# Third experts of two neighbouring tiles as seven block products, their sums kept in PSUM, in a fused attention and expert kernel

## The chip, the cores and the metric

One core of a Trainium2 chip runs the whole program. The metric is the time of one execution in microseconds on the device; of several runs the median counts.

## The reference

```python
def sm_attn(qq, kk, vv):
    s = scale * np.matmul(qq, kk.transpose(0, 1, 3, 2))
    s = s - np.max(s, axis=-1, keepdims=True)
    a = np.exp(s)
    a = a / (np.sum(a, axis=-1, keepdims=True) + 1e-09)
    return np.matmul(a, vv)
p_packed = sm_attn(p, k, v)
out = sm_attn(q, p_packed, p_packed)
...
h = np.maximum(np.maximum(x @ w1, x @ w2), x @ w3)
return (h @ w_out).astype(np.float32)
```

There are 8 batches of 8 heads, 576 tokens and a head width of 64; p holds 32 packed queries per head. The attention's output, with its heads side by side, is the x (4608 tokens by 512) of the second part: three experts (512 by 768 each), their elementwise maximum, and an output matrix (768 by 512). Everything is float32.

## The kernel before, in words

**Products.** A float32 matrix is split into a high part that TensorE multiplies exactly and a low part (`hi`, `lo`); one product of two such matrices is three matmuls, hi by hi, lo by hi and hi by lo, added up in one bank of PSUM.

**The low rank.** x of a batch is A by P: A (576 tokens by 8 heads x 32 = 256) the weights of the second attention, P (256 by 512) the packed rows. So x @ w is A by (P @ w). P @ w for tile j, 128 columns of each expert, is the stage P, `project` (L444 to L500): 32 small matmuls (L459) into two banks r = 0, 1 of 3 x 128 columns. The product with A is the stage N, `layer_in` in the batches 0 and 1 and `layer_in_fast` (L535 to L577, matmuls in L543) in the batches 2 to 7. For one expert and one tile it has four block products: two halves r of the 256 by two halves of 288 tokens.

**Seven for eight.** In the fast batches the experts 0 and 1 of a tile share the blocks of A, so their eight products are written as seven with sums and differences of the blocks (Strassen's way): those of A are made once a batch (T, `th`, `tl`), those of P @ w by `combine` (L486) for every tile. The third expert has its four plain products: two into the bank `me`, two into `mf`. A tile so takes 11. Its five banks are joined to the maximum of both token halves by the stage E, `maximum_fast` (L579 to L609): three or four copies out of PSUM by ScalarE or VectorE (L148, L150), and six joins (L587), all on VectorE, into `r`, the tile pair's rows in SBUF.

**Layer-out.** H (`halves`, L664 to L683) makes hi, lo and differences of the pair's rows (`ya`, `yb`, `yc`), O (`layer_out_fast`, L784) multiplies them with `w_out` in seven products over 14 banks of nine matmuls, F brings them to SBUF and out. A pair is two neighbouring tiles; six tiles are three pairs.

**The attention.** Per batch: S scores of the packed queries, A softmax and turn, X spread, V values (L357) and their scaling by VectorE (L367), K: one transpose of the packed rows on TensorE (L372) and a copy of it (`pt`, L148), Q the second scores from `pt` (L386), B the second softmax, which gives A's hi and lo (`a2h`, `a2l`). P needs `pt` too.

**The order** is written by hand, in three lists of words: START (weights, batches 0 and 1, the beginning of 2), LOOP (once for each b = 2 to 6), LAST (batch 7). A word is a stage, its batch relative to b (left out in w, C, W, R), its tile or half, and perhaps an engine:

```python
            name = word.rstrip("vga")
            chosen[0] = word[len(name):] or None
            kind, x = name[0], [int(i) for i in name[1:]]
...
                next(begun[key], None)
```

Each word runs one step of its stage, up to the next yield. `v`, `g`, `a` put the step's operation on VectorE, POOL (GpSimd) or ScalarE where it has a choice; the joins have none. Every engine works its own queue in the order in which the words issue. k, v, q, w are loads, all on SP's queue. I and J set a number of filler units, matmuls of the identity on itself (`rouse`, L162), in front of the next product or at once.

**Memory.** PSUM has eight banks: two pairs for scores, values, projections, queries (`ps_big`), four single banks for layer-in and layer-out (`ps_moe`); the projections 3 and 4 of the fast batches take single ones. SBUF tiles share rings of 6, 8 and 21 places (NX, NB, NY), taken in the order in which they are asked for.

## Time and profile before

| | us |
|---|---|
| median of three runs | 459.67 |
| lowest, highest run | 457.22, 459.70 |
| span of the profiled execution | 454.8 |
| TensorE busy in it | 448.5 |
| VectorE, POOL, ScalarE busy | 389.0, 266.7, 253.7 |
| one batch of the loop | 52.66 |

The profile is one execution. An engine's busy time counts its instructions from start to end, so that where two overlap they count once; the groups by line add up single instructions and can be more. Matmuls are pipelined: one that lasts 0.30 us has its successor behind it after less. The stretch of a loop batch is read from the start of one batch's scores to the start of the next batch's. The profile's spans on POOL are rough.

### The profile page before, as it was taken

To read this page: it belongs to the slowest core of one execution; us is meant where nothing else is said; L and a number is where in the kernel's file an instruction comes from. 1 tells how busy PE (TensorE), PEld (TensorE's weight loads), DVE (VectorE), ACT (ScalarE), POOL (GpSimd) and SP (SyncE) were. 2 spreads that over 40 slices of the span, in tenths; PEclk is the share of its full clock that TensorE was granted. 3 is DMA by queue.
4 is the path that set the end of the run, shared out by engine and by line. 5 is a ranking of instruction groups with operands and counts; after the bars stand their busy time and mean duration, and the time that the engine had idled before them with its cause. 6 is when DMAs were issued, how large, how long until landed. Compare 5 with 4: busy or idle time off the path is not lost.

```text
span 454.8 us, 11856 instructions
## 1 busy us (share of the span) xinstructions
PE 448.5 (99%) x4616; PEld 391.0 (86%) x4616; DVE 389.0 (86%) x825; ACT 253.7 (56%) x552; POOL 266.7 (59%) x280
## 2 busy tenths in 40 slices
PE   8999999999999999999999999999999999999997
PEld 4467888899999888988899888998889888999897
DVE  1799997999998989887997889898898879977883
ACT  2786956674453547446483546655474464744540
POOL 0458775644617685746856486836856478553350
PEclk9999999999999999999999999999999999999999
DMA  8999937000435450163304551063502640020002
GB/s 315 398 386 370 330 66 275 2 0 1 140 109 169 111 178 1 61 208 90 128 0 134 161 144 48 27 203 81 175 1 79 192 95 4 1 105 1 1 2 104
DMA packets 35783, 55.68 MB, mean 122 GB/s; under 512 B 17296, under 2 KB 26512, under 8 KB 35728
## 3 DMA queue, kind: packets, MB, share of 16 engines
q1 hardware_dynamic: 35728, 54.93, 36.3%
q8 instruction: 36, 0.59, 0.5%
q14 instruction: 19, 0.16, 0.1%
HBM read 41.94 MB, written 9.44 MB: 113 GB/s over the span
## 4 chain that ended last, share of the span: by engine, by line
PE 82%; DMA 12%; SPq 3%; DVE 1%; ACT 1%; issue 1%; POOL 0%; POOLq 0%; DVEq 0%; ACTq 0%
PE mo L784 22%; PE mx L543 10%; PE me L543 9%; PE mo L707 7%; DMA wi<-in_wi 7%; PE mu L543 6%; PE pw L459 6%; PE mf L543 6%; PE mi L630 6%; PE my L543 3%; DMA q<-in_qt 3%; SPq L339 2%; DMA v<-in_va 2%; PE s L386 2%; PE av L357 2%; PE s L273 1%
## 5 line engine op out<-in xcount | busy, mean ns | idle before, releaser
L672 POOL TENSOR_TENSOR r<-r 128x288 f32<-128x288 f32 (+1 forms) x39 | 45.4, 1164 | 59.1 <-DVE r L672 22.9
L477 DVE SCALAR_TENSOR_TENSOR pl<-pw,ph 128x768 fp32r<-128x768 f32 (+1 forms) x61 | 46.7, 775 | 11.4 <-ACT ph L475 11.2
L486 POOL TENSOR_TENSOR pf<-pf 128x128 f32<-128x128 f32 x72 | 40.7, 576 | 10.1 <-ACT pf L469 6.8
L153 POOL TENSOR_TENSOR sl<-pf,sh 128x384 fp32r<-128x384 f32 x28 | 30.6, 1100 | 27.2 <-DVE sh L150 17.7
L630 PE MATMUL mi<-a2h,ph 128*128 128x288 f32 x144 | 44.1, 306 | 0.0
L630 PE MATMUL mi<-a2l,ph 128*128 128x288 f32 x144 | 42.5, 295 | 0.0
L630 PE MATMUL mi<-a2h,pl 128*128 128x288 f32 x144 | 42.4, 294 | 0.0
L475 ACT ACTIVATE ph<-pw 128x768 fp32r<-128x768 f32 (+1 forms) x61 | 40.0, 680 | 2.8 <-PE pw L459 1.9
L459 PE MATMUL pw<-w_sb,pt 64*32 64x384 f32 x768 | 39.1, 490 | 0.1
L469 ACT ACTIVATE pf<-pw 128x512 f32<-128x512 f32 (+1 forms) x48 | 22.3, 492 | 26.4 <-PE pw L459 26.3
L225 POOL TENSOR_TENSOR w_sb<-w_sb,wi 128x512 int32<-128x512 int32 x18 | 23.7, 1327 | 21.7 <-DVE w_sb L221 16.2
L543 PE MATMUL me<-a2h,ph 128*128 128x288 f32 x108 | 32.6, 302 | 0.0
L630 PEld LDWEIGHTS mi<-a2h,ph 128*128 128x128 f32 x144 | 27.0, 188 | 6.4 <-issue 3.0
L784 PE MATMUL mo<-ych,xh 128*128 128x288 f32 x108 | 32.1, 298 | 0.0
L784 PE MATMUL mo<-ych,xl 128*128 128x288 f32 x108 | 31.9, 295 | 0.0
L543 PE MATMUL me<-a2h,pl 128*128 128x288 f32 x108 | 31.8, 294 | 0.0
L543 PE MATMUL me<-a2l,ph 128*128 128x288 f32 x108 | 31.8, 294 | 0.0
L784 PE MATMUL mo<-ycl,xh 128*128 128x288 f32 x108 | 31.8, 294 | 0.0
L148 ACT COPY r<-me 128x288 f32<-128x288 f32 x35 | 14.2, 405 | 25.1 <-PE me L543 25.1
L630 PEld LDWEIGHTS mi<-a2l,ph 128*128 128x128 f32 x144 | 27.0, 188 | 0.1
L630 PEld LDWEIGHTS mi<-a2h,pl 128*128 128x128 f32 x144 | 27.0, 188 | 0.0
L648 DVE TENSOR_TENSOR r<-mi,r 128x288 f32<-128x288 f32 x48 | 20.6, 447 | 3.1 <-PE mi L630 2.0
(216 smaller groups left out, 1669.9 us busy)
## 6 DMA issues: line engine op xcount, KB each, us to landing
kt<-in_kp SPq DMA_DIRECT2D x16, 640.0 KB, 5.1
...
```

The costliest lines, as they stand in the source:

```text
L153: on(default).tensor_tensor(out=lo, in0=src, in1=hi.bitcast(F32), op=ALU.subtract)
L225: nc.gpsimd.tensor_tensor(out=dst.bitcast(I32), in0=dst.bitcast(I32), in1=up, op=ALU.add)
L459: nc.tensor.matmul(out=ps[r][NP * n:NP * n + NP, 0:NW * P], lhsT=pt_sb[b % 2][o, NP * n:NP * n + NP], rhs=w_sb[o, j, n * NW * P:(n + 1) * ...
L469: nc.scalar.activation(out=f[:, r], in_=x[:, :, 0:2 * P], func=AF.Copy, scale=2.0 ** -WS)
L475: nc.scalar.activation(out=hi[:, r], in_=x, func=AF.Copy, scale=2.0 ** -WS)
L477: nc.vector.scalar_tensor_tensor(out=lo[:, r], in0=x, scalar=2.0 ** -WS, in1=hi[:, r].bitcast(F32), op0=ALU.mult, op1=ALU.subtract,)
L486: on("g").tensor_tensor(out=f[:, k], in0=f[:, x], in1=f[:, y], op=op)
L543: nc.tensor.matmul(out=ps[:, 0:HS], lhsT=w[wi], rhs=x[xi], start=first and n == 0, stop=n == 2, skip_group_check=not first,)
L630: nc.tensor.matmul(out=sums[b, j, hf, x][:, 0:HS], lhsT=w[:, r, x * P:(x + 1) * P], rhs=a[:, c], start=(r == 0 and n == 0), stop=(r == R - ...
L672: less = lambda out, x, y: on("g").tensor_tensor(out=out, in0=x, in1=y, op=ALU.subtract)
L707: nc.tensor.matmul(out=ps[:, 0:HS], lhsT=w[:, x, m * P:(m + 1) * P], rhs=h[:, z], start=(p == 0 and i == 0), stop=(p == NQ - 1 and i == 2),)
L784: nc.tensor.matmul(out=ps[:, 0:HS], lhsT=w[:, x, m * P:(m + 1) * P], rhs=h[:, z], start=(not onto and p == 0 and i == 0), stop=(p == NQ - ...
```

## The change

What it does, part by part:

1. **Products.** The third experts of the two tiles of a pair go together: their 2 x 2 blocks (tile by half r) times A's blocks are seven products instead of eight (`layer_in_thirds`, M). A tile's own products are the seven of its experts 0 and 1. `project_fast` leaves the parts for it, `thirds` (L) makes the combinations, `maximum_thirds` (D) joins the sums into both tiles' rows.
2. **Projections.** In the fast batches all projections take a pair of banks. The `pf` copy of 512 columns on ScalarE and the three combinations from it are gone: ScalarE copies one block of 128 (`f[:, 3]`), and VectorE makes the combinations from PSUM with the scaling in it (`onto`). hi and lo come in two pieces, 512 columns for the experts 0 and 1 and 256 for the third.
3. **Sums in PSUM.** `maximum_fast` copies the bank x to a bank e of its own, on which the products then go on adding; x goes on too. In D two of the sums are written by VectorE to PSUM, over a bank that was read.
4. **Places.** PSUM is one tile of eight banks; which bank a product takes, and which place in SBUF a tile takes, stands in written strings (HOMES).
5. **Lists.** START, LOOP and LAST are new. The weights of the thirds get replaced by differences of two tiles (R6 to R8) beside those of R0 to R5.

The lists' lines below are single lines of long lists.

```diff
-NX, NB, NY = 6, 8, 21
...
-k00 k01 I10 S0 A00 A00 J9 A00 q00 A00a w00 A01 A01 v00 J6 A01 v01 Z01 C00 C00 Z00 w02 C02 A01v V00 C00 V00 q01
-V01 V01 J2 K0 C00 w01 w10 K0a C02 C02 J2 Q0 B010 C02 B010 B010v C01 C01 w11 B010 C10 C01 C01 Q0 w12 C10 B001
...
+I10 k00 k01 S0 A00 A00 J8 A00 A01 A00v w00 C00 C00 A01 J3 J5 A01 A01a C00 C00 Z00 Z01 v01 w10 C10 v00 J3 V01 w02
+C02 V01 q00 C10 C10 C02 C02 q01 C02 C10 w12 C12 C12 w11 w32 V00 V00 K0 K0v J2 Q0 B000 B000 B000g B000 w01 C11 Q0
...
-P05g E03 E03 E03 P04g P05g P04g Q1 P04g k20 E04a N04 B10 E04a P04g P04g H03a N04 N04 H01g N04 N04 V101 B10
-B10g E04 E04a N05 E05a N04 N04 P10 B11 E04 A10 E04 P05v P12 N05 N05 E04 E04 B10 B10 P05g P10 E04 P05g P05 B11
...
+E05 M02 D02 M02 D02 M02 D02 E04 D02 E04 M02 M02 v11 D02 N05 E05 H03a V101 M02 H01a D02 D02 V101 D02 K1 K1a H05a
+D02 H04v H04a H01v H03g H03g P12 P12 Q1 B10 H04g O0 P12 P12 B11 P12 P12 H03g H03a F0 B11 O0 F0 O0 F0 P12 H05g O0
+O0 B10 B10v H05v H05g B11v B10 F0 O0 B10 B11 B10a P12 k20 H03g H05a P12 P12 B11 B11a F0 P11 B11 B10 P10 H05g
...
-E05 H03a N05 E05 H02g O0 N05 E05 E05 H05a O0 O0 O0 F0 F0 F0 H05v H05v H01g H01v F0 H03g O0 H03g P05 H03v H01v
...
+E05 D02 D02 D02 H04v H04v H04v H03g H03v H02g H02g O0 H05a H05v H03g H03v H05g F0 H05v H03g O0 O0 F0 F0 H01v
+H01v O0 O0 F0 F0 O0 O0 H03v H05v H05g H01a H01v F0 O0 O0 F0 F0 F0 O0 F0 O0 O0 F0 F0 O0 O0 F0 F0
...
-    ps_big = ctx.enter_context(tc.tile_pool(name="ps_big", bufs=2, space=PSUM))
-    ps_moe = ctx.enter_context(tc.tile_pool(name="ps_moe", bufs=4, space=PSUM))
+    psum = ctx.enter_context(tc.tile_pool(name="ps", bufs=1, space=PSUM)).tile([P, 8, 512], F32, name="psum")
+
+    def banks(name, n):
+        i = "abcdefgh".index(next(homes["ps"]))
+        return psum[:, i:i + n] if n > 1 else psum[:, i]
...
-        if j == 0 and b == 0 or j in (3, 4) and b >= 2:
+        if j == 0 and b == 0:
...
+    def project_fast(b, j, x):
+
+        p, i = j // 2, j % 2
+        c = [slice(k * P, (k + 1) * P) for k in range(NW)]
+        f = pool.tile([P, 4, P], F32, name=f"pf{b}_{j}", **home("y"))
+        scaled(f[:, 3], x[:, 1, c[1]])
+        yield 1
+        hi, lo = [pool.tile([P, R, 2 * P], F32R, name=f"p{n}{b}_{j}", **home(f"p{n}")) for n in "hl"]
+        pw[b, j] = (hi, lo)
+        scaled(hi, x[:, :, 0:2 * P])
+        yield 1
+        if (b, p) not in tw:
+            tw[b, p] = [[pool.tile([P, 2, R, P], F32R, name=f"q{n}{b}_{p}", **home("y")) for n in "hl"]]
+            third[b, p] = pool.tile([P, 4, P], F32, name=f"pt{b}_{p}", **home("b"))
+        t = third[b, p]
+        q = [y[:, i] for y in tw[b, p][0]]
+        scaled(q[0], x[:, :, c[2]])
+        yield 1
+        if i == 0:
+            scaled(t[:, 0::2], x[:, :, c[2]])
+        else:
+            scaled(t[:, 3], x[:, 1, c[2]])
+        yield 1
+        onto(f[:, 1], x[:, 0, c[1]], f[:, 3], -1, ALU.add)
+        yield 1
+        onto(lo, x[:, :, 0:2 * P], hi.bitcast(F32), 1, ALU.subtract)
+        yield 1
+        onto(f[:, 0], x[:, 0, c[0]], f[:, 1], 1, ALU.add)
+        yield 1
+        onto(f[:, 2], x[:, 1, c[0]], f[:, 1], 1, ALU.subtract)
+        yield 1
+        onto(q[1], x[:, :, c[2]], q[0].bitcast(F32), 1, ALU.subtract)
+        yield 1
+        if i == 1:
+            onto(t[:, 1], x[:, 0, c[2]], t[:, 3], -1, ALU.add)
+            yield 1
+        hi = pool.tile([P, 3, P], F32R, name=f"sh{b}_{j}", **home("y"))
+        copy(hi, f[:, 0:3])
+        yield 1
+        lo = pool.tile([P, 3, P], F32R, name=f"sl{b}_{j}", **home("y"))
+        split_lo(lo, f[:, 0:3], hi)
+        sw[b, j] = (hi, lo)
...
+            x, y = w(2 * (j - NJ), 2), w(2 * (j - NJ) + 1, 2)
+        on("g").tensor_tensor(out=y, in0=x, in1=y, op=ALU.subtract)
+        yield 0
+
+    def thirds(b, p):
+
+        f = third[b, p]
 
         def combine(k, x, y, op):
             on("g").tensor_tensor(out=f[:, k], in0=f[:, x], in1=f[:, y], op=op)
 
-        combine(1, 3, 1, ALU.subtract)
-        yield 1
         combine(0, 0, 1, ALU.add)
         yield 1
         combine(2, 2, 1, ALU.subtract)
         yield 1
-        hi = pool.tile([P, 3, P], F32R, name=f"sh{b}_{j}", tag="y", bufs=NY)
-        copy(hi, f[:, 0:3])
-        yield 1
-        lo = pool.tile([P, 3, P], F32R, name=f"sl{b}_{j}", tag="y", bufs=NY)
-        split_lo(lo, f[:, 0:3], hi)
-        sw[b, j] = (hi, lo)
-        yield 1
-
-    def replace(j):
-
-        w = w_sb[0:64, j].rearrange("p (n i x) -> p n i x", n=4, i=NW)
-        on("g").tensor_tensor(out=w[:, :, 1], in0=w[:, :, 0], in1=w[:, :, 1], op=ALU.subtract)
-        yield 0
+        y = pool.tile([P, 2, 3, P], F32R, name=f"sq{b}_{p}", **home("yt"))
+        copy(y[:, 0], f[:, 0:3])
+        yield 1
+        split_lo(y[:, 1], f[:, 0:3], y[:, 0])
+        tw[b, p].append(y)
...
+    def layer_in_thirds(b, p):
+
+        a = lambda r, i: [x[:, i, r] for x in tw[b, p][0]]
+        s = lambda i: [tw[b, p][1][:, k, i] for k in range(2)]
+        v, t = tokens(b)
+        x = block(b, f"X{p}")
+        product(x, a(0, 0), v(0, 0), first=True)
+        yield 0
+        u = block(b, f"U{p}")
+        product(u, a(0, 1), t(0, 1), first=True)
+        yield 0
+        product(x, s(1), t(1, 1))
+        yield 0
+        product(sums[b, f"E{p}"], a(1, 0), v(1, 0))
+        yield 0
+        product(u, a(1, 1), t(1, 0))
+        yield 0
+        product(x, s(0), t(0, 0))
+        yield 0
+        product(x, s(2), v(1, 1))
...
-        copy(h[0], of("e"))
-        yield 0
-        copy(of("e"), of("x"))
+        of = lambda name: sums[b, f"{name}{j}"][:, 0:HS]
+
+        copy(block(b, f"e{j}")[:, 0:HS], of("x"))
         yield 0
         copy(h[1], of("u"))
         yield 0
         join(h[1], of("y"), h[1])
         yield 0
-        u = pool.tile([P, HS], F32, name=f"u{b}_{j}", tag="y", bufs=NY)
-        copy(u, of("x"))
+        copy(h[0], of("x"))
+        yield 0
+        join(h[0], of("u"), h[0], ALU.add)
         yield 0
         join(h[0], of("e"), h[0])
         yield 0
-        join(u, of("u"), u, ALU.add)
-        yield 0
-        join(h[0], u, h[0])
-        yield 0
         join(h[1], of("x"), h[1], ALU.add)
         yield 0
-        join(h[1], of("f"), h[1])
+
+    def maximum_thirds(b, p):
+
+        h = lambda: hidden[b, p]
+        of = lambda name: sums[b, f"{name}{p}"][:, 0:HS]
+        q = pool.tile([P, 2, HS], F32, name=f"q{b}_{p}", **home("y"))
+        copy(block(b, f"E{p}")[:, 0:HS], of("X"))
+        yield 0
+        copy(q[:, 1], of("U"))
+        yield 0
+        copy(q[:, 0], of("X"))
+        yield 0
+        join(h()[:, 0], of("E"), h()[:, 0])
+        yield 0
+        join(of("E"), of("X"), q[:, 1], ALU.add)
+        yield 0
+        join(of("U"), of("U"), q[:, 0], ALU.add)
+        yield 0
+        join(h()[:, 2], of("U"), h()[:, 2])
+        yield 0
+        join(h()[:, 3], of("E"), h()[:, 3])
+        yield 0
+        join(h()[:, 1], of("X"), h()[:, 1])
```

Three places in the instruction queues, before and after. The number behind a name is only a buffer's; 128x288 is the shape written, x2 two such rows in a row.

TensorE, the end of batch 4's layer-in in the loop, where values, packed rows, projection and queries of batch 5 stand. Before (L357 values, L543 layer-in, L372 transpose, L386 queries):

```order
L357 MATMUL av_4043<-v_3792,xt_4010 32x64 x2
L543 MATMUL mf_3_4086<-a2h_0_3636,ph_3_3882 128x288
L543 MATMUL mf_3_4086<-a2h_0_3636,pl_3_3883 128x288
L543 MATMUL mf_3_4086<-a2l_0_3638,ph_3_3882 128x288
...
L543 MATMUL mf_3_4086<-a2l_1_3659,ph_3_3882 128x288
L372 MATMUL av_4043<-ident,pp_4100 128x128
L543 MATMUL me_4_4107<-a2h_0_3636,ph_4_4094 128x288
L543 MATMUL me_4_4107<-a2h_0_3636,pl_4_4095 128x288
L543 MATMUL me_4_4107<-a2l_0_3638,ph_4_4094 128x288
L543 MATMUL me_4_4107<-a2h_1_3654,ph_4_4094 128x288
...
L386 MATMUL s_5_0_4127<-q_4098,pt_74 32x288 x4
L386 MATMUL s_5_0_4127<-q_3848,pt_74 32x288 x4
```

After (L399 values, L632 layer-in, L414 transpose, L501 projection, L428 queries, L908 layer-out):

```order
L399 MATMUL psum<-v_3989,xt_3863 32x64 x2
L632 MATMUL psum<-a2h_1_3491,sq_2_3900 128x288 x2
L632 MATMUL psum<-a2l_1_3510,sq_2_3900 128x288
L414 MATMUL psum<-ident,pp_4046 128x128
L501 MATMUL psum<-w_sb,pt_72 32x384 x8
L428 MATMUL psum<-q_3673,pt_72 32x288 x4
L428 MATMUL psum<-q_3732,pt_72 32x288 x4
...
L908 MATMUL psum<-yah_0_3734,xh_1123 128x288
L908 MATMUL psum<-yah_0_3734,xl_1124 128x288
L908 MATMUL psum<-yal_0_3794,xh_1123 128x288
```

Before, six matmuls of layer-in stood between the values and the transpose and nine between the transpose and the queries, some of them left out here; after, there are three and none, the projection that reads `pt` stands directly behind the transpose, and layer-out begins behind the queries.

VectorE, the end of the last batch's layer-in (r_2 are the last pair's rows, u_5 a sum in SBUF, psum any bank, q_2 the third's sums). Before:

```order
L587 TENSOR_TENSOR r_2_6462<-my_5_6526,r_2_6462 128x288
L150 COPY u_5_6540<-mx_5_6516 128x288
L153 TENSOR_TENSOR yal_2_6545<-r_2_6462,yah_2_6543 128x576
L587 TENSOR_TENSOR r_2_6462<-me_5_6509,r_2_6462 128x288
L587 TENSOR_TENSOR u_5_6540<-mu_5_6522,u_5_6540 128x288
L587 TENSOR_TENSOR r_2_6462<-u_5_6540,r_2_6462 128x288
L587 TENSOR_TENSOR r_2_6462<-mx_5_6516,r_2_6462 128x288
L587 TENSOR_TENSOR r_2_6462<-mf_5_6570,r_2_6462 128x288
```

After:

```order
L687 TENSOR_TENSOR psum<-psum,q_2_6293 128x288
L687 TENSOR_TENSOR r_2_6248<-psum,r_2_6248 128x288
L687 TENSOR_TENSOR psum<-psum,q_2_6293 128x288
L687 TENSOR_TENSOR r_2_6248<-psum,r_2_6248 128x288 x6
L796 TENSOR_TENSOR r_2_6248<-r_2_6248 128x288
L192 CAST yah_2_6350<-r_2_6248 128x576
L195 TENSOR_TENSOR yal_2_6352<-r_2_6248,yah_2_6350 128x576
```

Before, a difference for `yal` stood among the last tile's joins, since the first tile's rows were final by then; after, all joins of the pair, the subtraction (L796), the cast and the difference for `ya` follow one another.

SP, the loads at the start (kt keys, q queries, wi weights, v values). Before:

```order
L178 DMA kt_79<-in_kp 128x1280
L178 DMA kt_81<-in_kp 128x1280
L193 DMA q_122<-in_qt 128x1152
L172 DMA wi_0_127<-in_wi 128x512
L184 DMA v_136<-in_va 128x1024
L185 DMA v_136<-in_vb 64x256
L184 DMA v_149<-in_va 128x1024
L185 DMA v_149<-in_vb 64x256
L172 DMA wi_2_160<-in_wi 128x512
L193 DMA q_189<-in_qt 128x1152
```

After:

```order
L220 DMA kt_77<-in_kp 128x1280
L220 DMA kt_79<-in_kp 128x1280
L214 DMA wi_0_121<-in_wi 128x512
L226 DMA v_147<-in_va 128x1024
L227 DMA v_147<-in_vb 64x256
L214 DMA wi_0_150<-in_wi 128x512
L226 DMA v_153<-in_va 128x1024
L227 DMA v_153<-in_vb 64x256
L214 DMA wi_2_177<-in_wi 128x512
L235 DMA q_182<-in_qt 128x1152
L235 DMA q_188<-in_qt 128x1152
```

Both query pieces of batch 0 now stand behind the values and three weight pieces (the second wi_0 and wi_2 are pieces of w1 and w0); before, one stood behind the keys and the other behind the values and w02.

## Rows read from the trace of the kernel before

**Rows 1.** The page, part 1: busy time, share of span, instructions of each engine.
```profile
PE 448.5 (99%) x4616; PEld 391.0 (86%) x4616; DVE 389.0 (86%) x825; ACT 253.7 (56%) x552; POOL 266.7 (59%) x280
```

**Rows 2.** The page, part 2: GB/s in 40 equal slices of the span.
```profile
GB/s 315 398 386 370 330 66 275 2 0 1 140 109 169 111 178 1 61 208 90 128 0 134 161 144 48 27 203 81 175 1 79 192 95 4 1 105 1 1 2 104
```

**Rows 3.** Table by batch: stretch, length, each engine's occupied time, clock, DMA share, GB/s.
```profile
300.24:352.90 52.66, 52.66 (x566) 46.70 (x565) 46.58 (x100) 29.59 (x68) 33.74 (x37) 1.00 0.34 105
```

**Rows 4.** Chain of waits in order of time: start, length, work.
```profile
320.52 1.39 PE av L357 x80
...
324.20 1.13 PE s L386 x32
...
329.50 1.45 PE pw L459 x32
...
334.77 0.81 PE pw L459 x16
...
436.13 15.48 PE mo L784 x117
```

**Rows 5.** Timeline of TensorE, stretch 203.7 to 206: start, length, instruction.
```profile
203.76 0.30 PE L543 MATMUL mf<-a2h,pl 128*128 128x288 f32 x1
203.89 0.29 PE L543 MATMUL mf<-a2l,ph 128*128 128x288 f32 x1
204.12 1.52 PE L459 MATMUL pw<-w_sb,pt 64*32 64x384 f32 x32
205.57 0.40 PE L543 MATMUL me<-a2h,ph 128*128 128x288 f32 x1
205.81 0.30 PE L543 MATMUL me<-a2h,pl 128*128 128x288 f32 x1
```

**Rows 6.** Timeline of the start: batch 0's packed rows, then a row of fillers.
```profile
14.84 0.28 DVE L367 TENSOR_SCALAR pp<-pa,r 128x64 f32<-128x64 f32 x1 [0.52 <-PE pa L357]
...
15.21 0.30 PE L372 MATMUL pa<-ident,pp 128*128 128x128 f32 x1
...
15.54 0.27 ACT L148 COPY pt<-pa 128x128 f32<-128x128 f32 x1 [0.58 <-PE pa L372]
...
15.87 0.96 PE L386 MATMUL s<-q,pt 64*32 64x288 f32 x24
...
20.78 4.78 PE L162 MATMUL idle<-ident 128*128 128x512 f32 x12
```

**Rows 7.** Groups by line and shape: busy us, mean ns | idle before.
```profile
L477 DVE SCALAR_TENSOR_TENSOR pl<-pw,ph 128x768 fp32r<-128x768 f32 x35 | 32.9, 943 | 4.8 <-ACT ph L475 4.6
...
L153 POOL TENSOR_TENSOR yal<-r,yah 128x576 fp32r<-128x576 f32 x14 | 20.8, 1484 | 4.1 <-ACT yah L148 3.3
...
L587 DVE TENSOR_TENSOR r<-u,r 128x288 f32<-128x288 f32 x36 | 18.9, 525 | 0.6
...
L477 DVE SCALAR_TENSOR_TENSOR pl<-pw,ph 128x384 fp32r<-128x384 f32 x26 | 13.7, 550 | 6.6 <-ACT ph L475 6.6
...
L150 DVE CAST yah<-r 128x576 fp32r<-128x576 f32 x1 | 0.5, 460 | 0.0
```

**Rows 8.** Timeline of VectorE in the batch of rows 3.
```profile
304.38 0.46 DVE L587 TENSOR_TENSOR u<-mu,u 128x288 f32<-128x288 f32 x1
304.87 0.46 DVE L587 TENSOR_TENSOR r<-u,r 128x288 f32<-128x288 f32 x1
...
322.16 0.47 DVE L367 TENSOR_SCALAR pp<-av,r 128x64 f32<-128x64 f32 x2
...
334.69 0.75 DVE L153 TENSOR_TENSOR yal<-r,yah 128x576 fp32r<-128x576 f32 x1
335.36 0.45 DVE L587 TENSOR_TENSOR r<-u,r 128x288 f32<-128x288 f32 x1
335.73 0.45 DVE L587 TENSOR_TENSOR r<-mx,r 128x288 f32<-128x288 f32 x1
```

**Rows 9.** Waits of VectorE: waiting, waited for: us, times, longest.
```profile
DVE pl L477 <- ACT ph L475: 11.2, 22, 0.7
```

More of the change, by code (lines that the diff above doesn't have):

```diff
@@ L265, in scores @@
         kt = [loaded.pop(("k", b, g)) for g in range(G)]
-        s1[b] = [ps_big.tile([P, 2, 512], F32, name=f"s1_{b}_{r}", tag="big") for r in range(R)]
+        s1[b] = [banks(f"s1_{b}_{r}", 2) for r in range(R)]
         rouse(s1[b][0][:, 0])
@@ L347, in values @@
         if (b, 0) not in av:
-            x = ps_big.tile([P, 2, 512], F32, name=f"av{b}", tag="big")
+            x = banks(f"av{b}", 2)
             for r in range(R):
@@ L466, in project @@
         if b >= FAST:
-            f = pool.tile([P, R, 2 * P], F32, name=f"pf{b}_{j}", tag="y", bufs=NY)
-            for r, x in zip(parts, src):
-                nc.scalar.activation(out=f[:, r], in_=x[:, :, 0:2 * P], func=AF.Copy, scale=2.0 ** -WS)
-                yield 1
-        hi = pool.tile([P, R, NW * P], F32R, name=f"ph{b}_{j}", tag="ph", bufs=3)
-        lo = pool.tile([P, R, NW * P], F32R, name=f"pl{b}_{j}", tag="pl", bufs=3)
+            yield from project_fast(b, j, x)
+            return
@@ L567, in layer_in_fast @@
         yield 0
-        product(e, a(1, 0), v(1, 0))
+        product(sums[b, f"e{j}"], a(1, 0), v(1, 0))
         yield 0
@@ L622, in layer_in @@
                 for x in new:
-                    sums[b, j, hf, x] = ps_moe.tile([P, 512], F32, name=f"mi{b}_{j}_{hf}_{x}", tag="moe")
+                    sums[b, j, hf, x] = banks(f"mi{b}_{j}_{hf}_{x}", 1)
                 rouse(sums[b, j, hf, i])
@@ L701, in layer_out @@
             x, y, z = PRODUCTS[n]
-            ps = sums[b, n, m] = ps_moe.tile([P, 512], F32, name=f"mo{b}_{n}_{m}", tag="moe")
+            ps = sums[b, n, m] = banks(f"mo{b}_{n}_{m}", 1)
             for p in range(NQ):
@@ L722, in temp @@
             if name not in tiles:
-                tiles[name] = pool.tile([P, 2, HS], F32, name=f"{name}_{b}", tag="y", bufs=NY)
+                tiles[name] = pool.tile([P, 2, HS], F32, name=f"{name}_{b}", **home("y"))
             return tiles[name]
@@ L778, in layer_out_fast @@
             else:
-                ps = sums[b, n, m] = ps_moe.tile([P, 512], F32, name=f"mo{b}_{n}_{m}", tag="moe")
+                ps = sums[b, n, m] = banks(f"mo{b}_{n}_{m}", 1)
             for p in range(NQ):
@@ L797, in finish_fast @@
             if into[n] not in tiles:
-                tiles[into[n]] = pool.tile([P, 2, HS], F32, name=f"{into[n]}_{b}", tag="y", bufs=NY)
+                tiles[into[n]] = pool.tile([P, 2, HS], F32, name=f"{into[n]}_{b}", **home("y"))
             x = tiles[into[n]]
```

233 lines of the change are left out of this document (132 added, 101 removed).

## The prediction

> **What bounds the kernel now.** I read the busy shares first, then the table by batch, then the chain, and only then single stretches. TensorE is busy 99% of a span of 454.8 us, VectorE 86%, POOL 59%, ScalarE 56% [rows 1], and its granted clock in the loop is 1.00 [rows 3], the upper of its two levels, 2.4 GHz. Busy matmuls overlap, so I checked that by spacing: in layer-in the 128x288 matmuls start 0.13 us apart, and the last 117 of the program take 15.48 us on the chain, **0.1323 us each** [rows 4, 5]. One batch of the loop, from its scores to the next batch's, lasts 52.66 us [rows 3], and the two before it last as long. Its work at these prices is 324 matmuls of 288 columns, 42.9 us; scores and queries 1.13 each, values 1.39; six projections in two pairs of 1.45 and two single ones of 0.81, 4.5 [rows 4]; and about 0.2 us for each of six excursions to small tiles: the gap before the projections is 0.23 instead of 0.13 and the one behind their first successor 0.24 [rows 5]. That makes 52.3 of 52.66, so TensorE loses some 0.3 us a batch to waits: it is the bound, and the change must be judged by what it does to TensorE's own queue. VectorE is the next engine, occupied 46.6 of the 52.66 us [rows 3].
>
> The sum is made against the profiled span of 454.8 us; the three runs lie 2.4 to 4.9 us above it, and I carry the difference onto their median, 459.67.
>
> **The change part by part.**
> *Products.* Before, a tile j takes 11 products of three matmuls, a pair of tiles 22. Now a tile takes 7 and the third expert of the pair 7 more: 21. One product for each of 3 pairs in 6 batches is 54 matmuls; 54 x 0.1323 = **-7.1 us**, all on TensorE, where nothing covers it. This is small because a product is short, not because it is hidden.
>
> *Fillers of the start.* The matmuls on the identity go from 63 to 56 units of 128 columns. 21 units took 4.78 us [rows 6], 0.228 each: **-1.6 us**. They stand where TensorE would wait anyway, so the gain could be nothing (if the wait takes their place); I take it and charge the wait next.
>
> *Queries of batch 0.* On SP's queue q00 moves from behind the keys to behind w00, v01, w10, v00 and w02, and up to the last query piece the queue carries one weight piece, w10, more: 512 KB. The first slices move 315 to 398 GB/s [rows 2], so this is about 1.4 us. Between 0 and +1.4, **+0.6 us**, since the 31 units of filler ahead of the queries (29 before) cover 0.5 of it.
>
> *Excursions.* From the end of the fillers to the loop TensorE leaves the 288-column matmuls 14 times before and 8 times now (single transposes not counted). Six x 0.2 = **-1.2 us**; in the loop there are 6 before and 6 now. Bounds 0 and -1.8.
>
> *Turn to layer-out, each loop batch.* Before, six matmuls stand between the values and the transpose of the packed rows, nine between the transpose and the queries that need its copy. Now three, and none: the copy is followed at once by a projection that reads it. Rows of the start show this chain bare: the last scaling begins at 14.84 and takes 0.28, the transpose starts at 15.21, the copy at 15.54, its reader at 15.87 [rows 6]. So transpose to reader is 0.66 us, where a matmul would have followed in 0.13 to 0.23: 0.43 to 0.53 lost. Ahead of it the two scalings take 0.47 [rows 8], begin some 0.1 behind the values and are followed by another 0.1 (14.84 + 0.28 to 15.21); against that stand three matmuls, the first of them behind small tiles, some 0.5: about 0.2 lost. 0.65 x 5 batches = **+3.3 us**; bounds 2.0 (part of it fell on waits that exist) and 5.0 (VectorE still has joins queued ahead of the scalings, 0.37 each [rows 8]). Behind it the same delay pays for something: the last pair's rows are final only when the third expert's last join is done, then one subtraction, a cast, and a difference on POOL of 1.48 us [rows 7] must be ready for the ninth matmul of layer-out. With projection and queries in between it comes about when it is needed, so I add nothing.
>
> *The last batch.* There is no next batch to put in between. Layer-out starts one product after the last third; six joins, a subtraction, a cast and a difference stand in a row on VectorE. Behind the last product some two joins (0.37 each), 0.48 for a dependent subtraction [rows 8] and 0.46 for a cast [rows 7] are ahead of the seventh matmul, which TensorE reaches in 0.8: 1.0 lost; the difference of 0.75 [rows 8] costs up to 0.5 more. **+1.0 us**, bounds 0.5 and 2.5.
>
> *VectorE.* Six projections of a batch: eight differences (4 of 943, 4 of 550 ns) and 6 of its 18 combinations (128 columns) become 6 of 512 columns, 6 of 256, 18 combinations and 3 + 3 for the thirds of 128. The differences give 157 ns + 1.02 per column [rows 7], so 681, 419 and 290: +5.8 us. Joins: 42 of 0.45 [rows 8] for 30 of 0.45 and 6 of 0.525 [rows 7]: +2.2. Splits, casts and copies that go to POOL and ScalarE less those that come back: -4. Together 99 instructions of 52.1 us become 122 of 56.2. An instruction's time overlaps its successor's by 52.1 - 46.6 = 5.5 us a batch, 0.055 each, so occupied time goes from 46.6 to **49.4 us** of some 52.1. That is 95%, with 2.7 us of waiting left where it had 6.1. It costs nothing only if the waits shrink; most are of the kind that may (VectorE there was ahead and waited for a product or for ScalarE's first cast, 0.5 us a time [rows 9]). I price it at 0 and keep it for the range and a rival.
>
> The VectorE page of the Trainium skill ("VectorE: DVE Perf Modes", The DRAIN you can't avoid) says the next operation does not start until the pipe has emptied. Independent joins here start 0.37 us apart while each lasts 0.45, a dependent pair 0.49 apart [rows 8], so the trace agrees for dependent pairs only. By the rule VectorE would need all 56.2 us a batch, which is the last rival below.
>
> *POOL and ScalarE* go from 34 to 38 and from 34 to 39 us of durations a batch, far from 52; their new work costs nothing unless late at the turn. Writing sums to PSUM instead of SBUF has no row before; the nearest, a join from PSUM, is 0.45 [rows 8], and I take that whatever its output; a PSUM output dearer by 0.1 would be 0.6 us a batch on VectorE, a cheaper one a gain as small, both within the range.
>
> **Sum:** -7.1 - 1.6 + 0.6 - 1.2 + 3.3 + 1.0 = **-5.0**: a span of 449.8, and **454.6 us** for the median, 1.1% faster. A difference of 1% (4.6 us) is about what a measurement of this kernel can tell from none, so the forecast lies just beyond it.
>
> **The rivals.**
> 1. *Full gain.* The turns are covered (the projection's wait falls on weight loads, or VectorE is ahead): only products, fillers and excursions count, -9.9, so 449.8. For it: TensorE loses 0.3 us a batch now, so such waits have been kept out before. Against: the bare chain of the start. Chance 0.18.
> 2. *The turns eat it.* 1.0 a batch, 2.5 at the end, nothing from the start: -7.1 + 5.0 + 2.5 = +0.4, 460; with half of the start's gain 458.6. I take 458.6. For it: POOL's 1.48 us difference stands last in that chain, and VectorE has less room to be early. Chance 0.30.
> 3. *VectorE sets the pace: slower.* If its 6.1 us of waiting a batch stay, a batch is 49.4 + 6.1 = 55.5, +2.8; times 6, +17, less 2.2 from the start: 474. It decides once its waits stay above 52.66 - 49.4 = 3.3 us. For it: every projection now strings dependent small operations after ScalarE. Against: its added work is spread, and many of today's waits are its being early. Chance 0.08.
> 4. *VectorE empties between operations.* 56.2 a batch, +3.5 x 6 - 2.2: 478. Against it stand the 0.37 us of [rows 8]. Chance 0.02.
> That the products don't go away is excluded: layer-in's list has one product a pair less.
>
> **The numbers.** Forecast 0.42, in its own bounds 452 to 457. Range: from 449 (rival 1) to 461 (rival 2's upper end), which leaves out rivals 3 and 4 and some misjudged start, 0.15 together. Faster by over 1% (below 455.1): rival 1 and 0.7 of the forecast, with a little of rival 2, 0.52. Within 1%: 0.38. Slower: rivals 3 and 4, 0.10.
>
> **What would show it.** A loop batch of 52.1 us instead of 52.66; layer-in with 1134 matmuls still 0.13 apart; a gap of about 0.5 us between the transpose of the packed rows and the projection behind it; a wait of about 1 us on the last yah or yal of the last batch; VectorE occupied about 49 us a batch; the first layer-in matmul near 26 us. A batch near 51.5 speaks for rival 1, above 52.7 for rival 3, where TensorE's waits would name VectorE's joins all over the batch. I would be wrong above all if many small waits of TensorE on VectorE, which no row of before shows, add up in the loop.

## The result and the profile after

The changed kernel took **461.65 us** (median of eight runs, 459.57 to 462.29), the kernel before 457.65 in the eight runs beside them: a ratio of 1.0078, 95% interval 1.0058 to 1.0099. The forecast was 454.6, faster by 1.1%; it is slower by 0.8%. (The forecast stood on the median of three runs, 459.67, which is 2.0 above that of the eight; as a change, -5.0 us was forecast and +4.0 measured.) The profiled executions differ alike, 459.5 us of span against 454.8.

The page of the changed kernel, part 1, answers [rows 1]:

```profile
PE 444.5 (97%) x4556; PEld 385.1 (84%) x4556; DVE 408.0 (89%) x958; ACT 270.8 (59%) x639; POOL 304.7 (66%) x279
```

TensorE has 4 us less to do and is busy 97% instead of 99%: the products are gone and more than their time has come back as standing still. Where, the table by batch shows (stretch, length, occupied time of TensorE, weight loads, VectorE, ScalarE, POOL, clock, DMA share, GB/s), each stretch from the scores of one batch to those of the next. Before:

```profile
141.65:194.85 53.20, 52.94 (x567) 47.00 (x566) 47.58 (x101) 29.90 (x69) 37.06 (x42) 1.00 0.37 111
194.85:247.51 52.66, 52.66 (x566) 46.85 (x565) 46.26 (x100) 29.66 (x68) 34.35 (x37) 1.00 0.34 105
247.51:300.50 52.99, 52.99 (x567) 47.01 (x566) 47.10 (x101) 29.77 (x68) 33.69 (x37) 1.00 0.35 105
300.50:353.37 52.87, 52.87 (x567) 46.91 (x566) 46.79 (x100) 29.77 (x68) 33.74 (x37) 1.00 0.34 104
```

The stretch of [rows 3] begins inside layer-in, 0.26 us ahead of the scores at 300.50, and its 52.66 us is the length of the shortest of these four batches; their mean is 52.93. The same of the changed kernel, which answers [rows 3]:

```profile
143.55:195.72 52.17, 51.71 (x557) 45.89 (x556) 49.17 (x126) 34.06 (x86) 41.42 (x40) 1.00 0.36 112
195.72:248.14 52.42, 52.06 (x557) 45.97 (x556) 49.09 (x123) 32.79 (x83) 36.81 (x35) 1.00 0.35 105
248.14:301.45 53.31, 52.12 (x557) 45.94 (x556) 49.09 (x123) 34.10 (x86) 36.84 (x35) 1.00 0.33 104
301.45:354.40 52.95, 52.29 (x557) 45.95 (x556) 49.23 (x123) 33.54 (x84) 36.81 (x35) 1.00 0.35 104
```

The +4.7 us of span fall into three parts: up to the scores of batch 3 +1.9 (141.65 to 143.55), four loop batches -0.9 (211.72 to 210.85), from there to the end +3.7. The forecast had -2.2, -2.1 and -0.7. The boundary is not quite the same in both kernels: LOOP began with two products of layer-in (N00) and then the scores (S1), and now begins with the scores, so that before, six matmuls, 0.9 us, stood ahead of it that now stand behind it. TensorE before:

```profile
141.42 0.29 PE L543 MATMUL me<-a2l,ph 128*128 128x288 f32 x1
141.65 1.20 PE L273 MATMUL s<-kt 64*32 64x288 f32 x32
```

Like for like, the start is +2.8, the loop -0.9 and the end +2.8.

**Loop.** The first batch is as short as forecast (52.17), the third is not. Timeline of TensorE there, at the scores of batch 5 (start, length, instruction, and in brackets the idle time before it and what ended it):

```profile
248.14 0.69 PE L315 MATMUL psum<-kt 64*32 64x288 f32 x8
249.67 1.18 PE L315 MATMUL psum<-kt 64*32 64x288 f32 x24 [0.84 <-DMA kt<-in_kp]
```

The scores stop after their first key piece and wait for the second. SP's timeline ahead of it shows why it is late:

```profile
226.72 0.33 SPq L220 DMA_DIRECT2D kt<-in_kp  x1
242.65 0.40 SPq L937 DMA_DIRECT2D out_t<-s  x1
244.04 0.40 SPq L937 DMA_DIRECT2D out_t<-u  x1
244.48 0.47 SPq L220 DMA_DIRECT2D kt<-in_kp  x1
```

Between the two key loads now stand two output stores, which wait for sums of layer-out; the second load goes out 3.7 us ahead of its scores (248.14). Before, both were issued in a row 31 us ahead of theirs (247.51):

```profile
216.28 0.89 SPq L178 DMA_DIRECT2D kt<-in_kp  x2
```

**The last batch.** The chain of waits of the changed kernel in order of time, from the last thirds on:

```profile
433.92 1.07 PE psum L632 x8
...
435.08 0.47 DVE r L687
...
435.58 1.92 DVE r L687 x5
...
437.52 0.47 DVE r L796
...
438.02 0.47 DVE yah L192
...
438.53 0.85 PE psum L908 x2
```

TensorE starts layer-out, stops at 436.28 and goes on 2.25 us later: six joins, a subtraction and a cast stand in a row. Then it is slow. Its table in two stretches there:

```profile
436.00:439.00 3.00, 1.04 (x7) 0.80 (x5) 2.83 (x8) 0.67 (x1) 0.60 (x1) 0.91 0.00 0
439.00:442.00 3.00, 2.99 (x13) 2.64 (x13) 3.00 (x5) 0.41 (x1) 1.24 (x1) 0.52 0.00 0
```

The granted clock is at its lower level, 1.2 GHz, for 3.41 us from 438.48 on, half of which, 1.7 us, is lost to TensorE.

**The start.** Waits of TensorE up to the scores of batch 3 (waited for, us in all, times, longest); before, one for the identity of 1.4, two of 0.2 and this one stood there:

```profile
PE s L386 <- DMA q<-in_qt: 1.0, 1, 1.0
```

Of the changed kernel:

```profile
PE psum L204 <- POOL ident masks.py:199: 1.4, 1, 1.4
PE psum L399 <- DMA xt<-x: 1.0, 3, 0.5
PE psum L204 <- DVE a1t L192: 0.7, 1, 0.7
PE psum L428 <- DMA q<-in_qt: 0.6, 1, 0.6
...
PE psum L831 <- DVE ycl L195: 0.5, 1, 0.5
```

Left out are four more of 0.5, for a converted weight, keys, a scaling and a query's issue, and one of 0.2. So there is no single cause, but thirteen waits in nine lines of this view besides the identity's, 5.0 us where there were 1.4. Summed over the trace up to the scores of batch 3, the fillers take 1.9 us less than before and the 288-column matmuls 2.0 less (0.9 of it the six that moved), the waits 3.6 more, and the rows of small matmuls, in which most of these waits stand, another 2.1 (the queries alone 1.3).

### The profile page after: what moved, and what is told of

It reads as the page before. It is cut to its first block, busy times and chain, and to the rows that moved or that the text cites. A ratio compares the mean times of both kernels' runs of the same rounds, so it can differ in the third digit from the quotient of the medians.

```text
span 459.5 us, 11925 instructions
## 1 busy us (share of the span) xinstructions
PE 444.5 (97%) x4556; PEld 385.1 (84%) x4556; DVE 408.0 (89%) x958; ACT 270.8 (59%) x639; POOL 304.7 (66%) x279
## 4 chain that ended last, share of the span: by engine, by line
PE 75%; DMA 7%; DVE 7%; ACT 4%; POOL 3%; issue 2%; SPq 1%; POOLq 0%; DVEq 0%; ACTq 0%
PE psum L632 34%; PE psum L908 18%; PE psum L501 7%; PE psum L831 6%; PE psum L754 5%; DMA kt<-in_kp 3%; PE psum L399 2%; DMA wi<-in_wi 2%; PE psum L315 2%; DMA wi<-in_wo 2%; PE psum L428 1%; SPq L381 1%; POOL w_sb L267 1%; POOL r L796 1%; ACT ph L521 1%
## 5 line engine op out<-in xcount | busy, mean ns | idle before, releaser
L687 DVE TENSOR_TENSOR r<-psum,r 128x288 f32<-128x288 f32 x216 | 92.5, 451 | 10.1 <-PE psum L632 6.3
L796 POOL TENSOR_TENSOR r<-r 128x288 f32<-128x288 f32 (+1 forms) x44 | 52.3, 1191 | 50.3 <-DVE r L687 33.3
L190 ACT COPY r<-psum 128x288 f32<-128x288 f32 x85 | 34.1, 402 | 19.8 <-PE psum L632 11.7
L754 PE MATMUL psum<-a2h,ph 128*128 128x288 f32 x144 | 43.4, 301 | 0.0
L754 PE MATMUL psum<-a2l,ph 128*128 128x288 f32 x144 | 42.5, 295 | 0.0
L754 PE MATMUL psum<-a2h,pl 128*128 128x288 f32 x144 | 42.4, 295 | 0.0
L501 PE MATMUL psum<-w_sb,pt 64*32 64x384 f32 x768 | 40.1, 491 | 2.3 <-ACT pt L190 1.8
L524 DVE SCALAR_TENSOR_TENSOR pl<-psum,ph 128x512 fp32r<-128x512 f32 (+2 forms) x49 | 35.9, 733 | 1.3 <-ACT ph L521 1.1
L908 PE MATMUL psum<-ych,xl 128*128 128x288 f32 x108 | 31.9, 295 | 0.0
L908 PE MATMUL psum<-ycl,xh 128*128 128x288 f32 x108 | 31.7, 294 | 0.0
L908 PE MATMUL psum<-ych,xh 128*128 128x288 f32 x108 | 31.7, 294 | 0.0
```

Of the source, the lines that this page charges most:

```text
L190: e.copy(out=out, in_=src)
L501: nc.tensor.matmul(out=ps[r][NP * n:NP * n + NP, 0:NW * P], lhsT=pt_sb[b % 2][o, NP * n:NP * n + NP], rhs=w_sb[o, j, n * NW * P:(n + 1) * ...
L524: nc.vector.scalar_tensor_tensor(out=out, in0=x, scalar=sign * 2.0 ** -WS, in1=y, op0=ALU.mult, op1=op)
L687: nc.vector.tensor_tensor(out=out, in0=x, in1=y, op=op)
L754: nc.tensor.matmul(out=sums[b, j, hf, x][:, 0:HS], lhsT=w[:, r, x * P:(x + 1) * P], rhs=a[:, c], start=(r == 0 and n == 0), stop=(r == R - ...
L796: less = lambda out, x, y: on("g").tensor_tensor(out=out, in0=x, in1=y, op=ALU.subtract)
```

## The experiments

The diffs show the lines that matter; where an edit changes the order in which places are asked for, the strings of HOMES change with it and are left out. A ratio is to runs of the kernel before beside them on the same chip, whose medians are 457.1 to 457.7, so that ratios compare better than medians.

| run | median us | ratio to before, 95% |
|---|---|---|
| changed kernel | 461.65 | 1.0078, 1.0058 to 1.0099 |
| e1_keys | 458.19 | 1.0012, 0.9987 to 1.0037 |
| e2_last | 458.93 | 1.0033, 1.0012 to 1.0053 |
| e3_turn | 470.27 | 1.0280, 1.0252 to 1.0309 |
| e4_start | 462.21 | 1.0105, 1.0087 to 1.0124 |
| e5_products | 468.70 | 1.0262, 1.0224 to 1.0301 |
| e6_joins | 476.38 | 1.0436, 1.0404 to 1.0468 |
| e7_keys_last | 455.51 | 0.9965, 0.9951 to 0.9979 |
| e8_turn | 456.89 | 0.9984, 0.9967 to 1.0002 |
| e9_bytes | 454.92 | 0.9948, 0.9927 to 0.9968 |
| e10_before | 469.19 | 1.0261, 1.0215 to 1.0306 |
| e11_fewer | 456.13 | 0.9979, 0.9950 to 1.0008 |
| e12_end | 456.10 | 0.9978, 0.9959 to 0.9996 |

**e1_keys.** LOOP, in two of its lines:

```diff
-P12 k20 H03g
+P12 k20 k21 H03g
...
-P11a k21 F0
+P11a F0
```

> Edit: in LOOP the load of the second key piece of the batch after next (k21) stands directly behind that of the first (k20) on SP's queue, instead of behind two of the batch's output stores; every tile keeps its place. Theory A (TensorE loses its time at four places, one of them the scores that wait for late keys): in the changed kernel the matmuls of the scores lose 0.29, 1.20, 0.58 and 0.27 us in the scores of the batches 4 to 7; that goes, the loop batches come to 52.1 to 52.4 us, and the median falls from 461.65 by 2.3 to about 459.3. Theory B (VectorE, occupied 49.1 of 52.9 us, sets the pace of a batch, and TensorE's waits are where this shows): the wait moves to another place, batches stay at 52.9, the median within 0.5 of 461.65.

Measured: 458.19, the ratio 0.0066 lower, 3.0 us (2.8 in span). SP's timeline and the table by batch:

```profile
278.27 2.92 SPq L220 DMA_DIRECT2D kt<-in_kp  x2
294.16 0.40 SPq L937 DMA_DIRECT2D out_t<-s  x1
```

```profile
247.51:299.65 52.14, 51.78 (x557) 45.97 (x556) 49.05 (x123) 34.23 (x86) 36.85 (x35) 1.00 0.33 106
299.65:351.73 52.08, 51.62 (x557) 45.82 (x556) 49.11 (x123) 33.77 (x84) 36.90 (x35) 1.00 0.34 106
```

All four batches are now at 51.8 to 52.2 (143.52 to 351.73, mean 52.05). Theory A holds here: the wait was the load's place on SP's queue, and it did not move elsewhere. (In seven of the ten runs the mean granted clock was 0.992 to 0.996, and they took 457.7 to 459.8; in three it was 1.000, and they took 455.4 to 455.8.)

**e2_last.** In `layer_out_fast`, for the last batch alone:

```diff
+        ahead = ORDER_FAST[:4] if b == B - 1 else []
+        for n, m in ahead:
+            sums[b, n, m] = banks(f"mo{b}_{n}_{m}", 1)
+        for p in range(NQ - 1):
+            for n, m in ahead:
...
-            for p in range(NQ):
+            for p in range(NQ - 1 if (n, m) in ahead else 0, NQ):
```

> Edit: in the last batch the first four banks of layer-out take their matmuls for the pairs 0 and 1 first, 24 matmuls, and only then those of the last pair; same matmuls, same sums. Theory A: the wait of 2.0 us for the last pair's yah is covered by 18 matmuls more (2.4 us), and the half clock of 3.4 us that follows it in the changed kernel, worth 1.7 us, goes with it, since TensorE does not stand still before: 461.65 less 3.4 to 3.7, about 458.1. Theory A without the link of wait and clock (the clock falls there for another reason): the clock still falls to half for some 3.4 us, only 1.8 goes, 459.8. Theory B (VectorE sets the pace to the end): the wait moves on to the next operands, yal, ybh or ych of the last pair, and less than 1 us goes, 460.7 or more.

Measured: 458.93, the ratio 0.0045 lower, 2.1 us (1.0 in span). The two stretches of the last turn again:

```profile
436.00:439.00 3.00, 3.00 (x23) 2.85 (x22) 2.83 (x8) 0.67 (x1) 0.64 (x1) 1.00 0.00 0
439.00:442.00 3.00, 2.89 (x20) 2.43 (x19) 3.00 (x5) 1.54 (x4) 1.25 (x1) 1.00 0.00 0
```

The gap is gone and the clock stays at 1.00, so gap and clock are linked, as theory A said; the 2.1 us alone would not tell, since they are nearer the 1.8 forecast without the link. The mean granted clock of every run says the same: 0.996 or less in 28 of 34 runs of the six kernels whose traces show the gap (the changed one, e1, e3 to e6), and in 4 of 52 of the six that cover it (e2, e7 to e9, e11, e12). But VectorE has as much to do in the two stretches (2.83 and 3.00) as without the edit, and 1.4 us come back as two waits further on, on `ycl`:

```profile
PE psum L921 <- POOL ycl L195: 0.8, 1, 0.8
...
PE psum L921 <- DVE ycl L195: 0.6, 1, 0.6
```

**e3_turn.** LOOP, the words around the values and the transpose:

```diff
-E04 D02 E04 M02 M02 v11 D02 N05 E05 H03a V101 M02 H01a D02 D02 V101 D02 K1 K1a H05a
+E04 D02 E04 v11 V101 M02 M02 D02 V101 N05 E05 H03a K1 M02 K1a H01a D02 D02 D02 H05a
```

> Edit: in LOOP the values of the next batch stand three products earlier, the transpose of the packed rows one product before the end of layer-in, so that nine matmuls stand between values and transpose and three between the transpose and the projection (three and none in the changed kernel); the second value load stands as much earlier. Theory A: the 0.69 us from transpose to projection fall to about 0.13, five batches: 2.5 to 3 us less, 459.0; if the values then wait for their load, up to 0.5 a batch comes back. Theory B: what the turn gives is lost again at layer-out's first operands of the last pair, 461.65 within 0.7.

Measured: 470.27, and neither theory had that. The wait between transpose and projection is gone from TensorE's waits, but others stand there:

```profile
PE psum L414 <- DVE pp L409: 3.5, 6, 0.6
PE psum L908 <- DVE yah L192: 2.0, 1, 2.0
PE psum L315 <- DMA kt<-in_kp: 1.9, 2, 1.1
PE psum L908 <- POOL yal L195: 1.9, 5, 0.4
```

The transpose now waits 0.6 us a batch for the scalings, which stand behind joins on VectorE, and layer-out 0.4 for the last pair's `yal`; the batches are 53.6 to 55.8 us. The edit moved work on three queues at a time, and its sum is not taken apart further.

**e4_start.** START:

```diff
-P03 q10 q11 Q1
+P03 Q1
...
-w30 C21 A11 A11
+w30 q10 q11 C21 A11 A11
...
-P12 P12 P12 V201 N10 N12 N10 H04g
+P12 P12 P12 N10 N12 N10 V201 H04g
```

> Edit: in START the two query pieces of batch 1 are loaded behind w30 instead of directly ahead of the queries that need them, some 8 us earlier on SP's queue, and the values of batch 2 stand 18 matmuls of layer-in later on TensorE. Theory A: the two waits within the queries of batch 1 (1.8 us) and those ahead of and within the values of batch 2 (2.3 us) go, 461.65 less 3.5 to 4.1, about 457.8. Rival (the start is bound by what the DMA engines move, 313 to 399 GB/s there): the waits move to the weights' words that come behind the queries, less than 1 us goes.

Measured: 462.21, no gain: the rival's way. Timeline of ScalarE (copies of the turned weights `a1t`):

```profile
37.46 0.68 ACT L249 ACTIVATE wi<-wi 128x512 f32<-128x512 f32 x1 [1.35 <-DMA wi<-in_wi]
...
38.58 0.76 ACT L190 COPY a1t<-psum 128x512 f32<-128x512 f32 x2
...
40.33 0.76 ACT L190 COPY a1t<-psum 128x512 f32<-128x512 f32 x2
```

In the changed kernel these copies began at 37.09 and 38.88. The queries, put ahead, delay the weight piece behind them; its conversion stands on ScalarE ahead of the copies, and the values of batch 1 wait 1.7 us for those.

**e5_products.** `layer_in_thirds`:

```diff
         product(x, a(0, 0), v(0, 0), first=True)
+        product(x, a(0, 0), v(0, 0), first=True)
```

> Edit: in the changed kernel the first product of every pair's third expert is issued twice (the second starts its bank anew, so sums stay the same): 54 matmuls more, the number that the change saves. Theory A (TensorE's queue is the bound, and a product is worth its 3 x 0.1323 us wherever it stands): 7.1 us more, 468.8. Rival (part of the saved products only bought waits that were there anyway, so that the true worth of the saving is smaller): 3 to 5 us more, 465 to 467, since added products then cover waits.

Measured: 468.70, 7.05 more than the changed kernel (6.8 in span; by the ratios 8.4, give or take 2.0): 54 matmuls are worth some 0.131 us each, theory A.

**e6_joins and e10_before.** The same line in `maximum_fast` of the changed kernel and of the kernel before:

```diff
         join(h[0], of("e"), h[0])
+        join(h[0], of("e"), h[0])
```

> Edit: in the changed kernel one join of every tile (a maximum) is issued twice, 36 joins of 0.40 to 0.45 us more on VectorE, 2.4 to 2.7 us a batch, nothing else. Theory A (VectorE is occupied 49.1 of 52.9 us and is not the bound): most goes into its waits, and only what stands in the turn to layer-out shows, 0 to 3 us more, 461.7 to 464.7. Theory B (VectorE sets the pace): 2.4 to 2.7 a batch for six batches, 14 to 16 us more, 476 to 478.

> Edit: in the kernel before, one join of every tile (a maximum) is issued twice, 36 joins of 0.45 us more on VectorE, as in e6_joins. Theory A' (before the change VectorE had room, 6.1 us of waiting a batch, and the change used it up): 0 to 5 us more than the kernel before, up to 462. Theory B' (VectorE was a second bound already before, and the change added to a full engine): 12 to 16 us more, about 471, as e6_joins did to the changed kernel.

Measured: 476.38, 14.7 us more than the changed kernel (14.0 in span), and 469.19, 11.5 more than the kernel before beside it (457.64). Two loop batches of e6_joins, then two of e10_before:

```profile
198.00:252.23 54.23, 52.39 (x558) 46.09 (x557) 51.34 (x129) 33.14 (x83) 36.87 (x35) 1.00 0.33 101
...
307.80:362.63 54.83, 52.68 (x558) 45.96 (x557) 51.55 (x129) 33.53 (x84) 36.92 (x35) 1.00 0.34 102
```

```profile
200.06:254.37 54.31, 54.14 (x567) 47.29 (x566) 48.26 (x106) 29.77 (x68) 33.91 (x37) 1.00 0.34 102
254.37:308.46 54.09, 53.95 (x566) 47.14 (x565) 48.34 (x106) 29.78 (x68) 33.89 (x37) 1.00 0.33 102
```

B's number holds for the changed kernel, and B' nearly so for the one before: a batch grows by 2.1 us for 2.3 of occupied VectorE, and by 1.1 to 2.0 (mean 1.5) for 1.7. (The profiled execution of e10_before is the longest of its four runs, 14.2 us longer in span than the kernel before; 3.2 of that come ahead of the scores of batch 3, where a wait and a lower clock stand, shown below. The two runs with a mean clock of 1.000 took 467.1 and 468.0.) In e10_before VectorE still has 5.8 us of waiting a batch (54.09 less 48.34), as many as without the added joins, and yet they did not take them in: for these 36 joins, idle time of VectorE is no room in either kernel. The added join reads what its twin ahead of it wrote; one at another place was not tried.

**e11_fewer.** e7_keys_last without that join, so one of three experts' sums is missing from a part of the maximum.

```diff
-        join(h[0], of("e"), h[0])
-        yield 0
```

> Edit: e7_keys_last with one join of every tile left out (the bank e is not brought into the maximum, so the output isn't the reference's), 36 joins of 0.40 to 0.45 us less on VectorE, nothing else. Theory B'' (in the loop VectorE is a second bound beside TensorE): the batches come down from 52.05 towards TensorE's own work of 51.1 to 51.4, 455.5 less 3 to 6. Theory A'' (only TensorE bounds the loop now, and added joins cost because nothing was left, while fewer gain nothing): the batches stay within 0.2 of 52.05, the median less than 1.5 below 455.5.

Measured: 456.13 against 455.51. The batches are 51.82, 52.01 and 51.78 instead of 51.86, 52.19 and 52.10, with VectorE at 47.1 instead of 49.0:

```profile
195.37:247.19 51.82, 51.47 (x557) 45.88 (x557) 47.09 (x117) 33.21 (x83) 36.87 (x35) 1.00 0.34 107
```

A'' in the main: 1.9 us less work on VectorE a batch shorten a batch by 0.15 us in the mean (0.04 to 0.32), and the median not at all. In this order VectorE is as early as it needs to be, and not earlier. Whether fewer joins would have gained in the kernel before, no run shows.

**e7_keys_last.** The edits of e1_keys and e2_last.

> Edit: e1_keys and e2_last together. Theory A (separate waits of TensorE): what each gave adds up. e1_keys brought the ratio to the kernel before from 1.0078 to 1.0012, e2_last to 1.0033; together 1.0078 - 0.0066 - 0.0045 = 0.997, about 456.0 beside 457.3 for the kernel before. Rival (the second half of the last batch is VectorE's chain, and any time given to it from ahead is lost behind): no better than e1_keys alone, 1.000 to 1.002.

Measured: 455.51, ratio 0.9965: they add up, and this version is faster than both kernels. Its clock stayed at 0.999 to 1.000 in all five runs, and the three runs of e1_keys at 1.000 were as fast (455.4 to 455.8). So, as far as these few runs go, what e2_last's edit adds to e1_keys is the clock that does not fall, and little for the gap itself.

**e8_turn.** In `layer_out_fast`, and one word in LOOP:

```diff
+                if p == NQ - 1 and (n, m) == ORDER_FAST[0] and b < B - 1:
+                    yield 0
...
-V101 D02 K1 K1a H05a
+V101 D02 K1 O0 K1a H05a
```

> Edit: e7_keys_last, and in LOOP the first six matmuls of layer-out (pairs 0 and 1 of its first bank) stand between the transpose of the packed rows and the projection that needs its copy. Theory A: the 0.69 us between transpose and projection become 0.13 plus what the bank waits for its last join; VectorE keeps its order, so nothing else moves (this is where e3_turn failed: there the scalings stood in another place of VectorE's queue). Five batches by 0.4 to 0.55: 2.0 to 2.7 us below e7_keys_last. Theory B (the turn is paced by VectorE's joins, subtraction and cast, which set when layer-out's last pair can be multiplied): the time comes back as a wait on yah or yal of the last pair, less than 0.7 us below e7_keys_last.

Measured: 456.89, no gain on e7_keys_last; the loop batches are 52.07 in the mean, 52.08 there. TensorE's timeline:

```profile
278.39 0.33 PE L414 MATMUL psum<-ident,pp 128*128 128x128 f32 x1
278.48 0.38 PE L923 MATMUL psum<-yah,xh 128*128 128x288 f32 x1
...
279.44 0.88 PE L501 MATMUL psum<-w_sb,pt 64*32 64x384 f32 x16
...
281.46 0.29 PE L923 MATMUL psum<-yah,xl 128*128 128x288 f32 x1
281.86 0.40 PE L923 MATMUL psum<-yal,xh 128*128 128x288 f32 x1
```

Six matmuls cover the transpose's copy (the projection follows at once), but TensorE leaves the wide matmuls once more, and the last pair's `yal` comes 0.27 us too late (281.46 to 281.86 where 0.13 follow elsewhere): theory B.

**e9_bytes.** In `load_w`; the rest is as told:

```diff
-        nc.sync.dma_start(out=t, in_=wi[j, c] if j < NJ else wo[c])
+        a = 0 if j < 3 or (j, c) == (3, 2) else WC - WC // 8
+        nc.sync.dma_start(out=t[:, a:], in_=(wi[j, c] if j < NJ else wo[c])[:, a:])
```

> Edit: e7_keys_last, but of 14 weight pieces (those of the tiles 3 to 5 but one, and w_out) only an eighth is loaded and stands for the whole piece, so that the products of these weights are not the reference's; ScalarE's two conversions of a piece come in two instructions, all other work stays. 6.3 MB less move in the first 70 us. Theory D (the start is late because of the bytes: any load put ahead pushes another back, as in e4_start): TensorE's waits for the queries of batch 1 (1.2 us) and for xt and the weights (1.9 us in all) go, and the scores of batch 3 start at 140 to 141 us instead of 142.9; 455.5 less 2 to 3. Rival (SP's queue waits for places that the conversion frees, and loads behind it wait with it, whatever their size): the scores of batch 3 within 0.7 of 142.9, the median within 1 of 455.5.

Measured: 454.92, within the rival's 1 us of 455.5, and the scores of batch 3 at 141.50, between the two theories. In e7_keys_last they start at 142.93, and in all kernels with an unchanged START at 142.1 to 144.3, so 1.4 us is less than the spread of these. The waits for loads are gone, but the one for a converted weight has grown from 0.7 to 1.2 and one for `a1t` (0.8) has come. That bytes are a part of the start's loss is likely and not shown; inconclusive.

**e12_end.** LAST:

```diff
-H03g H03v H02g H02g O0
+H03g H02g H02g H03g O0
```

> Edit: e7_keys_last, and in LAST the difference ybl of the middle pair (1.0 us on VectorE) goes to POOL, behind that pair's yah and yal, where POOL has nothing to do for 2.8 us. Theory A (behind the last turn layer-out waits for a chain on VectorE: two differences for ybl, four subtractions, a cast, ycl): the chain ends 1.0 us earlier, and of the two waits for ycl in e7_keys_last, 0.8 and 1.0 us, together 0.9 to 1.8 go: 454.6 to 453.7. Rival (POOL's one difference of 1.6 us pushes its own subtraction and the cast of ych, and the chain only changes engine): within 0.5 of 455.5.

Measured: 456.10, 0.6 above e7_keys_last, so no gain: the rival's way. The last layer-out is 0.5 us shorter in the trace, which the medians don't show.

## Why the prediction was wrong

1. **Products, -7.1: right.** Put back, they cost 7.05 (e5_products; 8.4 by the ratios, within their interval).
2. **A missing term: SP's queue in the loop.** I followed the loads of the start and did not look where the loop's key load had moved. 3.0 us (e1_keys). With it undone, the loop batch is 52.05. That this meets the 52.1 of the forecast is luck: the 52.66 it was taken from was read as the length of three batches and is that of the shortest of four. Their mean is 52.93, so TensorE lost 0.6 us a batch and not 0.3, and from there the batch fell by 0.88 where 0.53 was forecast.
3. **The last batch, +1.0 with bounds 0.5 and 2.5: too small, twice.** I put two joins between the last product and the subtraction; the chain shows six, 2.4 us, of which five begin behind the last third. And I priced the wait alone: the 2.1 us lost in the gap bring 1.7 at the lower clock behind them. 3.8 together, above my upper bound; e2_last shows the link, though only 2.1 us of it come off in the medians and 1.1 in the trace of the last layer-out, since the rest is VectorE's own chain.
4. **The start, -2.2: wrong in sign, +2.8 like for like.** I took the fillers (-1.6) and the excursions (-1.2) as gains and charged one wait, for the queries of batch 0, of 0.6. Both gains stand in the trace (-1.9 and -1.1); the step that failed is the charge for waits. They are on loads, conversions and copies, 3.6 us more than before, and 2.1 more go in the small matmuls around them: 5.7 where 0.6 was put. The sign to look for, the first layer-in matmul near 26 us, came at 28.57. Moving two loads moved the wait (e4_start). Which of bytes and conversions sets it stays open (e9_bytes).
5. **Turn to layer-out, +0.65 a batch: right for the gap, too large in sum.** Transpose to projection is 0.69 us instead of 0.13, five times, as the rows of the start had it. But in e1_keys a batch is 0.88 shorter than before with nine matmuls, 1.19 us, less, so all that the new order adds is 0.31 a batch: layer-in, interrupted less often by small tiles, loses 1.07 us a batch to them where it lost 1.48 (the batches from 195.69 and 194.85, against 0.1323 a matmul). That the gap can't simply be covered (e3_turn, e8_turn) was not foreseen.
6. **VectorE: 49.4 us a batch forecast, 49.1 measured, and free as forecast; but for the wrong reason.** I thought of its 6.1 us of waiting as room. They are not: added joins cost most of their time even in the kernel before (e10_before). That the change's own additions cost nothing because the lists put each where its result was early enough is argued, from e11_fewer. Rival 3, with its 474, did not happen; its condition, waits that stay, did in e6_joins (54.23 less 51.34 is 2.9 us a batch, 3.3 in the same batch without the added joins). Nor did rival 4: independent joins start 0.37 us apart here too.
7. **Sums in PSUM:** VectorE 457 ns into PSUM against 451 into SBUF, ScalarE's copies 389 against 402, as assumed:

```profile
L687 DVE TENSOR_TENSOR r<-psum,r 128x288 f32<-128x288 f32 x216 | 92.5, 451 | 10.1 <-PE psum L632 6.3 <-ACT r L190 0.2
...
L687 DVE TENSOR_TENSOR psum<-psum,q 128x288 f32<-128x288 f32 x36 | 15.9, 457 | 1.1 <-PE psum L632 0.4
```

In sum: from the 449.8 of span that were forecast to 459.5 it is 9.7. The start makes 5.0 of it, the loop 1.2 (the keys' 2.6 in the traces, less 1.4 by which the loop was cheaper than forecast), the end 3.5, of which 2.8 are the last batch and 0.7 were not taken apart. Rival 2, at 458.6, was the nearest, but its turns were not what ate the gain.
